# Attention, then two feed-forward layers, on one core: attention's second and third step change places

## The chip, the cores and the metric

The kernel runs on one core of a Trainium2 chip. The core has five engines that run side by side: TensorE (PE: matmuls, with a weight load, PEld, before each), VectorE (DVE), ScalarE (ACT), GpSimd (POOL) and SyncE (SP, which here only issues DMAs). Each works through its own list of instructions in order and waits for the others by semaphores. The metric is the device time of one execution in microseconds (us).

## The reference

The first layer is causal attention with a bias from a running sum; `x` then goes through a gated layer with a maximum over three products, and through one with a product of two.

```python
B, H, S, D = 4, 8, 576, 64
scores = q @ k.T / sqrt(D)
cum = cumsum(maximum(s, 0))
scores = where(causal, -1e9, scores + minimum(-(cum_q - cum_k), 0))
attn = exp(scores - max); attn /= (sum(attn) + 1e-9)
x = (attn @ v) as 2304 tokens x 512
h = maximum(maximum(x @ w1, x @ w2), x @ w3)      # 512 x 768, three times
x = h @ w_out                                     # 768 x 512
x = ((x @ w_a) * (x @ w_b)) @ w_out2              # 512 x 1536, twice; 1536 x 512
```

## The kernel before

**Steps.** Attention is cut into eight steps: for each of the four batches a short step (queries and keys 0 to 255) and a long one (queries 256 to 575, keys 0 to 575). A step has four pairs of heads, p0 to p3. A pair's scores go through a chain of engines: PE writes them to one of two PSUM buffers (`ps_s`); DVE adds the mask and takes the row's minimum (L398); ACT takes the exponential and its sum (L405); DVE takes the reciprocal (L409, L410); POOL scales the rows (L415); PE transposes them (`ft`, `t`, `tj`); ACT copies them out (`PF`); PE multiplies by the values (`fpv`); ACT and DVE split the result into a rounded part and a remainder (`Xh`, `Xl`).

**Two kinds of scores.** In the first three steps of the order the scores are plain: one full fp32 matmul over 64 rows and two more that carry the bias (`f` and `fj`, line 466; a long step has per pair four `f` of 384 or 512 columns, and two halves `fj` of a tile that both heads share). In all other steps they are split (`s`, `sj`, lines 422 to 457): operands are rounded to fp32r, the remainders and the bias stand in further rows, and two fp32r matmuls make a score. The operands stand in `QA1`, `QA2`, `KB1`, `KB2`, of which there is one each, and are written for every pair by `split_qk`: `KB` rounded on ACT and subtracted on DVE (64x1152), `QA` on ACT, POOL and DVE (64x640). A pair's loads (`kraw`, `qvraw`, two buffers each) are asked for two pairs ahead, when the value product of a pair is done; the queries and values share one buffer.

**The gated layer as filler.** While attention runs, PE fills its time with the gated layer of earlier steps: 18 gate units (`g`, line 592, 12 matmuls each of 256 or 320 columns) and four output units (`o`, line 620, 18 matmuls each) for every step. They need the step's `X` and the 24 chunks of weights, each of which is loaded by SP (512 KB), turned from 64-bit into fp32 by ACT (L241) and DVE (L244, L245), rounded on POOL (`hg`, `ho`) and subtracted on DVE (`lg`, `lo`). Three staging buffers hold chunks on their way.

**What sets the order.** The program makes a list (`stream`) of pieces with positions: an attention step takes one unit of position, gate and output units, and weight conversions, have positions of their own. Pieces are emitted by position, with priorities, and a scheduler then fixes each engine's order. After attention comes the rest of the gated layer and the last layer (line 1086), with PE as its chief engine.

Of the kernel before, what the change touches and what calls it, by code (L numbers as in the profile page):

```python
# [9 lines left out]
F32R = mybir.dt.float32r  # L10
# [19 lines left out]
def kernel(  # L30
# [29 lines left out]
    P = 128  # L60
# [9 lines left out]
    NPLAIN = 3  # L70
# [198 lines left out]
    def fetch_w1(key):  # L269
        if key in w1_t:  # L270
            raw = wst.tile([P, WC, 2], I32, tag="wst", name="wraw")
        else:
            if key == w1_keys[NPRE - MF]:
                wst.release()
                w1o.append(
                    tc.alloc_tile_pool(name="w1o", bufs=1, side="left", reuse_waits="tile")
                )
            w1_tiles(w1o[0], [key])
            raw = w1o[0].tile([P, WC, 2], I32, tag="raw", bufs=1, name="wraw")
        if key[0] == "g":  # L280
            src = (w1, w2, w3)[key[1]][key[2]]
        else:
            src = wo[key[1]]
        fetch_w(raw, src)
        w1_raw[key] = raw
# [11 lines left out]

    def is_plain(b, R):


        return 2 * b + R < NPLAIN

# [335 lines left out]
    pairs = [(b, R, p) for b in range(B) for R in range(2) for p in range(NP)]  # L638
# [133 lines left out]
    def x_tiles(stp):  # L772
        if stp not in xt:
            while todo and todo[0][0] <= stp - 2 and todo[0][1] < 3 * MF:
                todo.pop(0)[2]()
            R = stp % 2
            n = N1 if R else Q0
            xt[stp] = [
                mp.tile([P, KC, n], F32R, tag=f"X{c}{R}", bufs=1, name=f"X{c}")
                for c in "hl"  # L780
            ]
        return xt[stp]
# [6 lines left out]
    M0, M1 = 0.7, 0.1  # L789
    W0, W1, W2 = (0.09, 0.27, 0.34, 0.38), 1.3, 1.8  # L790
    for stp in range(nsteps):
        b, R = divmod(stp, 2)
# [9 lines left out]
        tot = sum(c for c, _ in units)  # L802
        acc = 0.0
        m0 = stp + 1 + (M0 if stp == 0 else M1)
        m1 = stp + 2 + M1
        for n, (c, fn) in enumerate(units):
            todo.append((stp, n, fn))
            stream.append((m0 + (m1 - m0) * acc / tot + 1e-6, 0, m_next))
            acc += c
# [12 lines left out]
    ng = 3 * MF  # L822
    for j in range(ng):
        w_at = W0[j] if j < 3 else W0[3] + (W1 - W0[3]) * (j - 3) / (ng - 3)
        stream.append((w_at, 200, w_next))
    for j in range(MF):
        stream.append((W1 + (W2 - W1) * j / MF, 200, w_next))
    stream.sort(key=lambda e: e[0])
    for pos, off, fn in stream:
# [5 lines left out]
        else:  # L835
            fn()
    moe = [(1, m_next) for _ in range(len(todo))]
# [702 lines left out]
```

## Time and profile before

| what | value |
| --- | --- |
| median of 3 timed runs | 921.25 us (918.19 to 922.32) |
| the profiled execution's own time, and its span | 915.72 us, 913.9 us |
| PE busy | 900.2 us, 98% |
| DVE busy | 592.2 us, 65% |
| ACT busy | 378.9 us, 41% |
| POOL busy | 225.7 us, 25% |

The span is the profiled part; 1.8 us of that execution lie around it. PE counts as busy from the start of a matmul to its modelled end, and matmuls overlap in the pipeline, so a PE that waits a little between matmuls still shows as busy. What it really does is seen by the distance from one start to the next.

### The profile page before, as it was taken

The page shows a single profiled execution, that of the slowest core. Times are in us where ns is not written, and L with a number is a line of the kernel's source. Part 1 is how long each engine was busy: PE and PEld are TensorE (multiplying, and loading weights), DVE is VectorE, ACT ScalarE, POOL GpSimd, SP SyncE. Part 2 cuts the span into 40 slices and gives each one's busy share as a digit, 9 for nine tenths or more (in the row PEclk, how much of TensorE's full clock was granted, in tenths as well). Part 3 has the DMA queues.
Part 4 walks back from the last instruction along what each step waited for, and adds up shares of the span by engine and source line. Part 5 has one row for each costly group of instructions (what it writes and reads, how often), then busy time and mean ns, then how long its engine had stood idle before and what let it go on. Part 6 is the DMA issues. An engine that isn't in the chain of part 4 may idle for free.

```text
span 913.9 us, 17151 instructions
## 1 busy us (share of the span) xinstructions
PE 900.2 (98%) x6296; PEld 849.0 (93%) x6296; DVE 592.2 (65%) x1407; ACT 378.9 (41%) x879; POOL 225.7 (25%) x328
## 2 busy tenths in 40 slices
PE   7999999999999999999999999999999999999998
PEld 7677899989999989999899999999999998999998
DVE  4798535554465544555369567767675868996874
ACT  4665634555446564465433332322322222423321
POOL 6654302222123221232122102111111212321211
PEclk9999999999999999999999999999999999999999
DMA  5665332313223132221143214444443243254331
GB/s 169 224 202 175 90 87 73 98 42 101 70 85 97 43 91 80 85 85 54 41 149 134 88 53 155 152 150 145 144 159 107 107 146 122 77 165 158 117 116 47
DMA packets 55212, 102.36 MB, mean 112 GB/s; under 512 B 5736, under 2 KB 39432, under 8 KB 55128
## 3 DMA queue, kind: packets, MB, share of 16 engines
q1 hardware_dynamic: 50520, 96.54, 33.4%
q10 hardware_dynamic: 4608, 4.72, 1.6%
q8 instruction: 50, 0.82, 0.4%
q14 instruction: 34, 0.28, 0.1%
HBM read 77.29 MB, written 23.94 MB: 111 GB/s over the span
## 4 chain that ended last, share of the span: by engine, by line
PE 90%; DVE 4%; DMA 3%; issue 1%; SPq 1%; ACT 1%; POOL 0%; DVEq 0%; ACTq 0%; POOLq 0%
PE g L592 25%; PE X L1086 23%; PE Z L1086 11%; PE o L620 9%; PE Y L1086 6%; PE fpv L531 5%; PE t L545 3%; PE f L466 2%; PE s L422 2%; PE s L423 1%; DVE slot L897 1%; PE ft L508 1%; DMA wraw<-in_moe_w_dram 1%; PE tj L558 1%; PE sj L456 1%
## 5 line engine op out<-in xcount | busy, mean ns | idle before, releaser
L592 PE MATMUL g<-Xh,hg 128*128 128x256 f32 (+1 forms) x576 | 174.8, 305 | 0.5 <-ACT xo L625 0.5
L592 PE MATMUL g<-Xl,hg 128*128 128x256 f32 (+1 forms) x576 | 173.4, 301 | 0.0
L592 PE MATMUL g<-Xh,lg 128*128 128x256 f32 (+1 forms) x576 | 173.2, 301 | 0.0
L592 PEld LDWEIGHTS g<-Xh,hg 128*128 128x128 f32 x576 | 108.5, 189 | 4.4 <-issue 1.6
L592 PEld LDWEIGHTS g<-Xl,hg 128*128 128x128 f32 x576 | 108.9, 189 | 2.5 <-issue 1.4
L592 PEld LDWEIGHTS g<-Xh,lg 128*128 128x128 f32 x576 | 108.8, 189 | 1.2 <-issue 0.9
L1086 PE MATMUL X<-xh,wh 128*128 128x384 f32 x288 | 97.5, 339 | 1.5 <-ACT u L1127 0.6
L1086 PE MATMUL X<-xl,wh 128*128 128x384 f32 x288 | 96.9, 336 | 0.0
L1086 PE MATMUL X<-xh,wl 128*128 128x384 f32 x288 | 96.9, 337 | 0.0
L88 POOL TENSOR_SCALAR wh<-wval 128x256 fp32r<-128x256 f32 x84 | 41.5, 503 | 190.5 <-DVE wval L891 141.8
L1086 PE MATMUL X<-woh,slot 128*128 128x256 f32 x432 | 81.1, 281 | 0.5 <-ACT ob L1129 0.5
L415 POOL TENSOR_SCALAR P<-P,rs 128x128 f32<-128x128 f32 (+2 forms) x80 | 50.1, 631 | 91.4 <-DVE rs L410 75.0
L601 DVE TENSOR_TENSOR hf<-g,hf 128x256 f32<-128x256 f32 (+1 forms) x96 | 43.5, 453 | 41.5 <-PE g L592 39.4
L897 DVE TENSOR_TENSOR slot<-hraw,slot 128x768 fp32r<-128x768 f32 x60 | 60.5, 1031 | 14.9 <-POOL slot L88 13.7
L1086 PEld LDWEIGHTS X<-woh,slot 128*128 128x128 f32 x432 | 68.0, 189 | 0.7 <-ACT ob L1129 0.7
L897 DVE TENSOR_TENSOR u<-Z,u 128x384 f32<-128x384 f32 x72 | 39.6, 552 | 44.5 <-ACT u L1129 34.0
L405 ACT ACTIVATE P<-P,nm 128x128 f32<-128x128 f32 (+2 forms) x80 | 46.5, 582 | 32.7 <-DVE nm L398 27.1
L1086 PE MATMUL X<-wol,slot 128*128 128x256 f32 x216 | 60.1, 280 | 0.0
L620 PE MATMUL o<-hh,lo 128*128 128x256 f32 (+1 forms) x192 | 58.0, 306 | 0.0
L620 PE MATMUL o<-hl,ho 128*128 128x256 f32 (+1 forms) x192 | 57.8, 303 | 0.0
L620 PE MATMUL o<-hh,ho 128*128 128x256 f32 (+1 forms) x192 | 57.0, 302 | 0.3 <-ACT xo L625 0.3
L398 DVE CUSTOM_DVE_ANT_0 P<-s,maskJ 128x128 f32<-128x128 f32 (+2 forms) x80 | 40.5, 514 | 25.7 <-PE s L423 16.7
(165 smaller groups left out, 2255.9 us busy)
## 6 DMA issues: line engine op xcount, KB each, us to landing
hT<-u SPq DMA_DIRECT2D x72, 192.0 KB
hraw<-hT SPq DMA_DIRECT2D x36, 384.0 KB
wraw<-in_moe_w_dram SPq DMA_DIRECT2D x18, 512.0 KB
wraw<-in_moe_w_out_dram SPq DMA_DIRECT2D x18, 512.0 KB
qvraw<-in_qv_dram SPq DMA_DIRECT2D x12, 640.0 KB
kraw<-in_kT_dram SPq DMA_DIRECT2D x24, 288.0 KB
wraw<-in_moe_w_a_dram SPq DMA_DIRECT2D x12, 512.0 KB
wraw<-in_moe_w_b_dram SPq DMA_DIRECT2D x12, 512.0 KB
```

What stands on the lines that cost most here:

```text
L88: nc.gpsimd.tensor_scalar(o, i, scale, 1.0, op0=ALU.mult, op1=ALU.mult)
L398: nc.vector.tensor_tensor_reduce(pt[:, c0 : c0 + w], v_, m_, -scale, first, op0=ALU.add, op1=ALU.min, accum_out=nm[:, i : i + 1],)
L405: e_ = nc.scalar.activation(pt[:, c0:c1], pt[:, c0:c1], AF.Exp, bias=first, scale=-1.0, accum_out=sm[:, g : g + 1],)
L415: nc.gpsimd.tensor_scalar(pt[:, c0:c1], pt[:, c0:c1], rs[:, g : g + 1], 1.0, op0=ALU.mult, op1=ALU.mult,)
L422: nc.tensor.matmul(ps, QA1[:, qs], KB1[:, h, ksl], start=True, stop=False)
L531: nc.tensor.matmul(ps[h * D : h * D + D, c0:n], w, x, start=(t == 0), stop=(t == len(mm[h]) - 1),)
L545: nc.tensor.transpose(ps[:, j * P : j * P + P], pt[:, j * P : j * P + P], ident)
L592: nc.tensor.matmul(ps[:, :n], w[:, kk, :], x[:, kk, :], start=(i == 0), stop=(i == len(mm) - 1),)
L601: st["V"] = nc.vector.tensor_tensor(hf, ps[:, :n], hf, op=ALU.max)
L620: nc.tensor.matmul(ps[:, :n], w[:, c, :], x[:, m, :n], start=(i == 0), stop=(i == len(mm) - 1),)
L897: return {"V": nc.vector, "P": nc.gpsimd}[e].tensor_tensor(o, a, b, op=op)
L1086: nc.tensor.matmul(ps[:, :n], w, x, start=(first and i == 0), stop=(i == len(mm) - 1), skip_group_check=not first,)
```

## The change

The first four steps run in the order batch 0 short, batch 1 short, batch 0 long, batch 1 long (before: batch 0 short, batch 0 long, batch 1 short, batch 1 long). Plain scores are used for the two short steps alone, so batch 0's long step is now split like the other long steps. The buffers of `X` are named after the step's place in the list and not its kind, and each is 320 columns wide. Gate and output units of the first three steps get positions from a table (`FILL`), and the weight conversions stand at new positions: the fourth to sixth from 0.68 (before from 0.38), the next seven over the second step, the last eleven over the first half of the third. The last two weight chunks' staging buffer gets a pool of its own, which is released when attention ends.

```diff
-    NPLAIN = 3
@@ fetch_w1
-        if key in w1_t:
+        if w1_keys.index(key) < len(w1_keys) + NPRE - MF:
...
+                for nm in ("w1o", "w1r"):
...
     def is_plain(b, R):
-        return 2 * b + R < NPLAIN
+        return R == 0 and b < 2
...
-    pairs = [(b, R, p) for b in range(B) for R in range(2) for p in range(NP)]
+    steps = [(0, 0), (1, 0), (0, 1), (1, 1)]
+    steps += [(b, R) for b in range(2, B) for R in range(2)]
+    pairs = [(b, R, p) for b, R in steps for p in range(NP)]
...
-                mp.tile([P, KC, n], F32R, tag=f"X{c}{R}", bufs=1, name=f"X{c}")
+                mp.tile([P, KC, n], F32R, tag=f"X{c}{stp % 2}", bufs=1, name=f"X{c}")
...
-    M0, M1 = 0.7, 0.1
-    W0, W1, W2 = (0.09, 0.27, 0.34, 0.38), 1.3, 1.8
+    M1 = 0.1
+    FILL = [(1.05, 2.22, 2.45, 2.65), (2.65, 3.12, 3.12, 3.3), (3.3, 3.9, 3.9, 4.1)]
...
+        elif j < 6:
+            w_at = 0.68 + 0.105 * (j - 3)
+        elif j < 13:
+            w_at = 1.0 + 0.143 * (j - 6)
+        else:
+            w_at = 2.0 + 0.057 * (j - 13)
...
+    w1o[1].release()
```

The engines' lists show three places. First DVE, in the first short step, around the fourth weight conversion (`wraw`, whose load comes late): before, it stands between the first half of the sixth score tile, `F_431`, and the reciprocal of the tile before.

```order
L398 ISA F_431,nm<-f_430,maskJ 128x128
L398 ISA nm 128x1
L244 TENSOR_SCALAR wraw<-wraw 128x512
L410 RECIPROCAL rs<-rs 128x2
L92 TENSOR_TENSOR Xl<-fpv,Xh 128x256
L398 ISA F_431,nm<-f_430,maskJ 128x256
```

In the changed kernel the same tile is `F_408`, and the conversion's first instruction stands one tile later.

```order
L399 ISA F_408,nm<-f_407,maskJ 128x128
L399 ISA nm 128x1
L411 RECIPROCAL rs<-rs 128x2
L91 TENSOR_TENSOR Xl<-fpv,Xh 128x256
L399 ISA F_408,nm<-f_407,maskJ 128x256
L399 ISA nm 128x1
L91 TENSOR_TENSOR lg_0_147<-wraw,hg_0_146 128x512
L410 TENSOR_SCALAR rs<-sm 128x2
L399 ISA F_460,nm<-f_459,maskJ 128x128
L399 ISA nm 128x1
L411 RECIPROCAL rs<-rs 128x2
L243 TENSOR_SCALAR wraw<-wraw 128x512
```

The reciprocal, the remainder and the tile's second half have moved ahead of the conversion.

Second PE, in batch 0's long step, at the change from the third pair to the fourth. Before, the next pair's scores (`fj`) and the transposes stand among gate matmuls and need no operand of their own.

```order
L592 MATMUL g<-Xh,lg_5_175 128x256
L466 MATMUL fj<-kraw,qvraw 64x288 x2
L592 MATMUL g<-Xh,hg_5_174 128x256
L545 MATMUL t_958<-ident,F_894 128x128 x4
L592 MATMUL g<-Xl,hg_5_174 128x256
L592 MATMUL g<-Xh,lg_5_175 128x256
```

After, a pair's last scores (`s_1581`), few output matmuls and the last transposes stand ahead of the next pair's joint scores `sj`.

```order
L423 MATMUL s_1581<-KB_138,QA_140 128x384
L424 MATMUL s_1581<-KB_139,QA_141 128x384
L546 MATMUL t_1574<-ident,P_1491 128x128 x3
...
L546 MATMUL t_1600<-ident,P_1503 128x128 x4
...
L546 MATMUL t_1621<-ident,P_1537 128x128 x4
L457 MATMUL sj<-KB_138,QA_140 128x288
L458 MATMUL sj<-KB_138,QA_140 128x288
```

In the two gaps stand six and three output matmuls; the scores `sj` now read `KB` and `QA`, which must be rewritten after `s_1581`.

Third DVE, in the same step of the changed kernel, one pair earlier: `P_1315` is the last tile but one of the second pair, `KB` belongs to the third.

```order
L399 ISA P_1315,nm<-s_1312,maskJ 128x512
L399 ISA nm 128x1
L91 TENSOR_TENSOR Xl<-fpv,Xh 128x320
L411 RECIPROCAL rs<-rs 128x1
L91 TENSOR_TENSOR lo_183<-wraw,ho_182 128x512
L91 TENSOR_TENSOR KB_139<-kraw,KB_138 64x1152
L410 TENSOR_SCALAR rs<-sm 128x1
L399 ISA P_1347,nm<-s_1344,maskJ 128x384
L399 ISA nm 128x1
L411 RECIPROCAL rs<-rs 128x1
L243 TENSOR_SCALAR wraw<-wraw 128x512
L376 SCALAR_TENSOR_TENSOR QA_140<-qvraw,QA_140 64x2x320
```

The split of the operands and the weight conversions now stand in one list with the softmax of the same step; before, this step had no split.

## Rows read from the trace of the kernel before

**Rows 1.** Windows by stage: busy us and instructions of each engine, clock, DMA.

```profile
31.60:91.80 60.20, 60.04 (x397) 43.63 (x397) 52.99 (x156) 37.79 (x93) 31.51 (x40) 1.00 0.63 204
91.80:148.70 56.90, 56.90 (x408) 50.88 (x406) 25.69 (x93) 27.01 (x79) 13.24 (x24) 1.00 0.31 87
148.70:460.00 311.30, 311.30 (x2380) 289.16 (x2380) 158.93 (x516) 164.77 (x417) 75.74 (x114) 1.00 0.26 76
```

**Rows 2.** Timeline of PE in batch 0's long step: start, duration, instruction.

```profile
47.71 0.71 PE L466 MATMUL fj<-kraw,qvraw 66*64 66x288 f32 x4
48.34 0.39 PE L592 MATMUL g<-Xh,hg 128*128 128x256 f32 x1
...
50.11 0.28 PE L592 MATMUL g<-Xh,lg 128*128 128x256 f32 x1
50.23 0.28 PE L592 MATMUL g<-Xh,hg 128*128 128x256 f32 x1
...
53.95 1.02 PE L466 MATMUL f<-kraw,qvraw 66*128 66x512 f32 x2
54.80 0.39 PE L545 MATMUL t<-ident,F 128*128 128x128 f32 x2
```

**Rows 3.** Timeline of PE in batch 1's long step, whose scores are split.

```profile
154.18 0.40 PE L422 MATMUL s<-KB,QA 128*128 128x512 f32 x1
...
154.66 0.30 PE L592 MATMUL g<-Xh,hg 128*128 128x320 f32 x1
...
163.53 0.29 PE L456 MATMUL sj<-KB,QA 128*128 128x288 f32 x1
163.66 0.29 PE L457 MATMUL sj<-KB,QA 128*128 128x288 f32 x1
```

**Rows 4.** Groups of PE instructions, 31.6 to 91.7 us: count, busy, mean ns, idle.

```profile
L592 PE MATMUL g<-Xh,hg 128*128 128x256 f32 x72 | 21.7, 312 | 0.0
...
L545 PE MATMUL t<-ident,F 128*128 128x128 f32 x42 | 7.0, 275 | 0.2 <-POOL F L415 0.2
...
L531 PE MATMUL fpv<-PF,qvraw 128*64 128x320 f32 x24 | 4.6, 447 | 0.0
```

**Rows 5.** Timeline of all engines, 24 to 34 us; in brackets the idle time before.

```profile
27.89 0.43 DVE L244 TENSOR_SCALAR wraw<-wraw 128x512 int32<-128x512 int32 x1 [3.09 <-DMA wraw<-in_moe_w_dram]
...
28.23 0.16 DVE L410 RECIPROCAL rs<-rs 128x2 f32<-128x2 f32 x1
...
32.24 0.39 PE L592 MATMUL g<-Xh,hg 128*128 128x256 f32 x1
```

**Rows 6.** Groups of DVE instructions, 31.6 to 92 us: the weight conversions.

```profile
L245 DVE SCALAR_TENSOR_TENSOR wraw<-wraw 128x512 int32<-128x512 int32 x18 | 13.3, 739 | 0.7 <-ACT wraw L241 0.5
L92 DVE TENSOR_TENSOR lg<-wraw,hg 128x512 fp32r<-128x512 f32 x15 | 10.9, 725 | 1.9 <-POOL hg L88 1.6
L244 DVE TENSOR_SCALAR wraw<-wraw 128x512 int32<-128x512 int32 x18 | 9.1, 504 | 2.7 <-DMA wraw<-in_moe_w_dram 1.5 <-DMA wraw<-in_moe_w_out_dram 1.2
```

**Rows 7.** Groups of DVE instructions, 0 to 340 us: operand split and score rows.

```profile
L92 DVE TENSOR_TENSOR KB<-kraw,KB 64x1152 fp32r<-64x1152 f32 x8 | 11.4, 1425 | 4.8 <-ACT KB L81 4.8
L398 DVE CUSTOM_DVE_ANT_0 P<-s,maskJ 128x512 f32<-128x512 f32 x16 | 11.0, 690 | 6.1 <-PE s L423 3.8 <-PE tj L558 2.1
...
L375 DVE SCALAR_TENSOR_TENSOR QA<-qvraw,QA 64x640 fp32r<-64x640 f32 x8 | 7.6, 946 | 2.7 <-ACT QA L81 2.6
```

**Rows 8.** Timeline of all engines, 187 to 199 us: a pair's queries arrive.

```profile
187.69 2.42 PE L531 MATMUL fpv<-PF,qvraw 128*64 128x320 f32 x20
...
190.19 0.34 SPq L343 DMA_DIRECT2D qvraw<-in_qv_dram  x1
...
194.32 0.72 POOL L88 TENSOR_SCALAR QA<-qvraw 64x640 fp32r<-64x640 f32 x1 [4.09 <-DMA qvraw<-in_qv_dram]
```

**Rows 9.** Group of POOL instructions, 31.6 to 92 us: scaling of 512 columns.

```profile
L415 POOL TENSOR_SCALAR F<-F,rs 128x512 f32<-128x512 f32 x6 | 6.8, 1140 | 4.8 <-DVE rs L410 4.8
```

**Rows 10.** The same work on POOL, 340 to 460 us.

```profile
L415 POOL TENSOR_SCALAR P<-P,rs 128x512 f32<-128x512 f32 x8 | 6.1, 767 | 8.6 <-DVE rs L410 4.8 <-PE o L620 2.2 <-PE s L423 0.9
```

More of the change, by code (lines that the diff above doesn't have):

```diff
@@ L274, in fetch_w1 @@
                 wst.release()
[L275 to L279, printed above, removed]
+                for nm in ("w1o", "w1r"):
+                    w1o.append(
+                        tc.alloc_tile_pool(name=nm, bufs=1, side="left", reuse_waits="tile")
+                    )
+                    if nm == "w1o":
+                        w1_tiles(w1o[0], w1_keys[NPRE - MF :])
+            raw = w1o[1].tile([P, WC, 2], I32, tag="raw", bufs=1, name="wraw")
         if key[0] == "g":
@@ L775, in x_tiles @@
                 todo.pop(0)[2]()
-            R = stp % 2
-            n = N1 if R else Q0
+            n = N1 if steps[stp][1] else Q0
             xt[stp] = [
-                mp.tile([P, KC, n], F32R, tag=f"X{c}{R}", bufs=1, name=f"X{c}")
+                mp.tile([P, KC, n], F32R, tag=f"X{c}{stp % 2}", bufs=1, name=f"X{c}")
                 for c in "hl"
@@ L786, in m_next @@
             todo.pop(0)[2]()
-    M0, M1 = 0.7, 0.1
-    W0, W1, W2 = (0.09, 0.27, 0.34, 0.38), 1.3, 1.8
+    M1 = 0.1
+    FILL = [(1.05, 2.22, 2.45, 2.65), (2.65, 3.12, 3.12, 3.3), (3.3, 3.9, 3.9, 4.1)]
     for stp in range(nsteps):
-        b, R = divmod(stp, 2)
+        b, R = steps[stp]
         att = []
@@ L801 @@
         units = moe1_units(R, b, lambda stp=stp: x_tiles(stp))
[L802 to L805, printed above, removed]
+        m0 = stp + 1 + M1
+        g0, g1, o0, o1 = FILL[stp] if stp < 3 else (m0, m0 + 0.75, m0 + 0.75, m0 + 1)
+        ng = 3 * MF
         for n, (c, fn) in enumerate(units):
             todo.append((stp, n, fn))
-            stream.append((m0 + (m1 - m0) * acc / tot + 1e-6, 0, m_next))
-            acc += c
+            if n < ng:
+                at_ = g0 + (g1 - g0) * n / ng
+            else:
+                at_ = o0 + (o1 - o0) * (n - ng) / (len(units) - ng)
+            stream.append((at_ + 1e-6, 0, m_next))
     def tails():
@@ L820, in w_next @@
             load_w1(w1_pend.pop(0))
-    ng = 3 * MF
-    for j in range(ng):
-        w_at = W0[j] if j < 3 else W0[3] + (W1 - W0[3]) * (j - 3) / (ng - 3)
+    W0 = (0.09, 0.27, 0.34)
+    for j in range(len(w1_keys)):
+        if j < 3:
+            w_at = W0[j]
+        elif j < 6:
+            w_at = 0.68 + 0.105 * (j - 3)
+        elif j < 13:
+            w_at = 1.0 + 0.143 * (j - 6)
+        else:
+            w_at = 2.0 + 0.057 * (j - 13)
         stream.append((w_at, 200, w_next))
-    for j in range(MF):
-        stream.append((W1 + (W2 - W1) * j / MF, 200, w_next))
     stream.sort(key=lambda e: e[0])
```

## The prediction, made before the changed kernel ran

> **What bounds the kernel now.** I read the windows first. From 31.6 us on PE is busy nearly all the time, at a granted clock of 1.00 [rows 1]. Busy is not enough: in the pipeline a waiting PE still shows as busy. So I set the number of matmuls against the distance between starts. A gate matmul of 256 columns starts 0.12 us after the one before; a full fp32 score of 512 columns holds PE for 0.85 us (one of 384, by columns, 0.64), a half of the plain joint tile for 0.63 [rows 2]. From 31.6 to 91.7 us there are 216 gate matmuls (three groups of 72): 25.9 us. The group of transposes has 42, and 25 more are in three smaller ones: 67 at 0.11, 7.4 us. Six scores of 512, seven of 384 and eight joint halves make 5.1, 4.5 and 5.0. Two long value products (24 records of 320 columns, 12 each) take 2.4 each [rows 4, 8], two short ones together some 1.6. The sum is 54.3 us, and the stretch lasts 60.2 [rows 1]: PE loses 5.9 us there. DVE is busy for 52.99 of the 60.2 us, 88%, because of the weight conversions; in the next two windows it is busy for 45% and 51%, and there I take PE's losses as alike before and after. So the kernel is bound by PE's work, plus what PE waits in the first 92 us, plus a start in which it has little to do: the first gate matmul comes at 32.24 us [rows 5]. Any PE time saved without a new wait shortens the whole.
>
> **The change, part by part.**
>
> The scores of batch 0's long step. A pair now costs PE 2 x 0.64 + 2 x 0.85 + 2 x 0.63 = 4.24 us. Split, a score of 512 columns takes 0.48 (two matmuls), one of 384 then 0.36, and a joint half is four matmuls at 0.13, 0.53 us [rows 3]: 2 x 0.48 + 2 x 0.36 + 2 x 0.53 = 2.74. Four pairs: 4 x 1.5 = **6.0 us saved**. The Trainium skill, FP8 and Floating Point Precision, section TensorE Precision Notes, says that true fp32 goes through the array in four passes; counted so for each head, a joint half would take 2 x 4 x 288 columns at 2.4 GHz, 0.96 us, and the term would be an estimate of 8.7 us. The measured 0.63 decides: the two heads' halves are not counted one after the other.
>
> The start. In the first short step DVE sat idle for 3.09 us, until 27.89, before a weight conversion whose load had not landed; the reciprocal behind it ran at 28.23 [rows 5], and the remainder and a half tile behind that. In the new list they stand ahead of it. Not all of the 3.09 us comes back: on ACT the same conversion still stands ahead of the copy that the second pair's value product needs. Bounds 0 and 3.1; I take **1.3 us saved**, a little under the middle.
>
> The second short step, as filler's first home. Until batch 0's joint scores PE has 170 gate matmuls (20.4 us) and some 13 us of plain scores, transposes and value products. DVE has eight weight conversions in that time, each of three instructions, 0.74 + 0.73 + 0.50 less 0.08 for each, since the next one starts before the last one's record ends (28.23 against 27.89 + 0.43) [rows 5, 6]: 1.73 us, 13.8 together, and some 12.5 us of the rest. That is 80% of PE's 33 us, less than the 88% that went with a loss of a tenth. Waits between 0 and 3.3 us; I take 2.5, nearer to the stretch before.
>
> The long split step. This is where the gain can go. From the first pair's joint scores to the end of the output units PE has 46 gate and 72 output matmuls (14.2 us), scores (15 split ones and four joints, 10.6), 57 transposes (6.3) and three value products (7.3): 38.4 us. DVE has, by its list, nine weight conversions (15.6), three `KB` of 1.43 and three `QA` of 0.95 [rows 7], less the overlap 6.6; eight score tiles of 512 at 0.61, seven of 384 at about 0.48 and eight joint halves at about 0.41, 11.5; and some 6 us of reciprocals, remainders and gate maxima: 39.7 us. So DVE needs at least 1.3 us more than PE. At the 88% that it reached before, it needs 45.1, and PE waits 6.7. What is late next is seen by walking through the lists. There is one `KB` and one `QA`, so between a pair's last score and the next joint stand ACT's rounding and DVE's 1.43 us, and on DVE whatever is queued ahead; the reciprocals for the last tiles of the old pair are queued behind `KB`, so POOL's scaling and the last transposes wait for it too. Before, such a change was covered by many gate matmuls; now by nine output matmuls, 1.1 us, and transposes. At the third and fourth pair the queries add to it: their buffer is free when the value product two pairs back is done, and from the request (190.19) to the first use (194.32) is 4.1 us [rows 8], to which ACT's and DVE's `QA` add some 1.8, so 5.9; behind the second pair's value product PE has only 3.7 us of work. Adding up such waits with the durations above I get 4.4 us up to the first pair's value product, 1.8 at the third pair and 2.5 at the fourth, 8.7 in all; conversions are shorter when POOL is quiet, so I take **8.2**, between 1.3 and 11 (each of the eight last transposes and joints waiting 0.3 us longer).
>
> What I cost at nothing: the wider buffers of `X`, since the instructions use only the columns of the step; the plain loads of the second short step, which are smaller than those of the long one that they replace; the tail of the filler, since by the fourth step all eight steps' units stand where they stood. If the last is wrong, it would show as waits of PE after 150 us, where DVE is at 51% [rows 1]. The staging pool's release moves a buffer that nothing waits for there.
>
> The sum: -6.0 - 1.3 + (2.5 + 8.2 - 5.9) = -2.5 us, on the profiled execution's 915.72 us, so 913.2. That execution lies 5.5 us under the median of the timed runs, 921.25; by the same difference I predict **918.5** for the median, 0.3% less. About 0.5%, 4.6 us, is what a measurement of this kernel can tell from no change.
>
> **The rivals.**
>
> PE's waits stay small. The conversions leave the start, and DVE's 39.7 us need not bind if the scheduler has put into each gap what is ready: then the second short step loses 1 us and the long one 3, and the sum is -6.0 - 1.3 + (4 - 5.9) = -9.2, so 912. For it: before, PE lost only a tenth while DVE was 88% busy. Against it: then the step had no operands to rewrite. Between this and my sum lies a continuous scale; I give the half below about -4.6 us a chance of 0.35.
>
> The loads come late, and the change is slower. Queries, keys and weight chunks share SP's list, and a chunk's request there waits for a staging buffer that DVE frees; a pair's loads stand behind it. If each of the step's four joints waits 3 us longer than I have it, and the first value product after it, that is +13 us: 931. It decides when the step's waits pass 10.7 us, and by 0.5% at 15.3. For it: DMA engines are at 0.63 and 204 GB/s in the early window [rows 1], and the step asks for four pairs' full keys, queries and values besides nine chunks. Against it: that window fed DVE at the same rate with few waits for DMA in its groups [rows 6]. Chance 0.12.
>
> POOL and DVE slow each other. Scaling 512 columns took 1140 ns on POOL in the stretch where DVE was 88% busy, and 767 ns where it was not [rows 9, 10]. At the old pair's last transposes in the long step, which wait for POOL, it costs 0.37 us more than at the quiet rate at six tiles: +2 us, 920.5, no change still. The Trainium skill, GPSIMD Engine Reference, section 1. Specifications, says that GpSimd's SBUF interfaces are shared with VectorE; the trace agrees, with these two rows. I count it into the forecast's own range.
>
> That the change does not do what it says, with the scheduler putting the old order back, is out: the lists show `sj` in batch 0's long step.
>
> **How the numbers follow.** Forecast (a saving of 0 to 4.6 us, or a loss up to 3) 0.48; small waits 0.35; late loads 0.12; anything else, such as a change of the later steps by some us either way, 0.05. Faster by over 0.5%: small waits and a part of the rest, 0.38; slower by over 0.5%: late loads and a little, 0.13; within: 0.49. The forecast's own range is 916 to 922. The range for 8 in 10 leaves out the slower half of the late loads and the best of the small waits: 910.5 to 923.5.
>
> **What would show it.** In the changed kernel's profile: no `f` of 384 or 512 columns, and PE's groups of `s` and `sj` up by a third; the idle time of DVE before the fourth conversion gone, and the first gate at about 31 us; in the long step DVE at 85% or more and starts of PE further apart than 0.12 us at the joints of the second, third and fourth pair, with DVE's `KB` or `QA` as what came last. The prediction is wrong if that step's PE work takes 41 us or less (then it is the first rival), or 50 or more with waits for `qvraw` or `kraw`.

## The result, and the profile after

The changed kernel takes **927.77 us** (median of four, 927.55 to 929.16) where the kernel before took 920.22 beside it (918.19 to 922.32): ratio **1.0085**, interval 1.0058 to 1.0112. It is slower by about 7.5 us; 918.5 was forecast. Beside all later runs the kernel before took 917.0 to 917.7 us (medians), so this one ratio may be some 0.3% too low when it is set against those below. The two profiled executions lie 11.9 us apart (spans 925.8 and 913.9), and that distance is already there in batch 2's long step, whose second joint starts at 291.88 us and at 279.18 before.

Windows of the changed kernel, as in [rows 1]: length, busy us of PE, PEld, DVE, ACT and POOL, granted clock, DMA share, GB/s.

```profile
33.10:72.00 38.90, 36.26 (x276) 30.79 (x275) 34.26 (x102) 24.91 (x74) 20.98 (x30) 1.00 0.78 235
72.00:129.00 57.00, 47.34 (x300) 38.83 (x299) 43.84 (x127) 35.27 (x80) 25.16 (x30) 0.88 0.48 144
78.50:81.90 3.40, 3.40 (x14) 3.26 (x15) 3.27 (x7) 3.40 (x8) 3.04 (x3) 0.50 0.18 28
102.40:105.80 3.40, 3.27 (x15) 3.27 (x16) 2.09 (x7) 1.37 (x4) 1.32 (x3) 0.50 0.77 221
116.10:122.90 6.80, 5.61 (x24) 5.12 (x24) 4.13 (x12) 2.03 (x5) 1.41 (x3) 0.50 0.39 99
129.00:150.00 21.00, 21.00 (x173) 19.68 (x173) 9.58 (x29) 10.07 (x24) 3.33 (x5) 1.00 0.31 93
150.00:460.00 310.00, 310.00 (x2333) 289.34 (x2332) 156.31 (x502) 162.40 (x411) 72.22 (x110) 1.00 0.25 71
```

The first row is the second short step, the second is batch 0's long step to the end of the output units. The reader is to see three things. PE is idle for 9.7 us of the long step, where [rows 1] had it busy throughout. VectorE is busy for 43.84 of 57 us, 77%: it isn't the bound there. And TensorE's clock, 1.00 in every window of [rows 1], is granted at 0.50 (1.2 GHz instead of 2.4) in three stretches inside it.

Groups of PE, DVE and POOL in the long step (72 to 129 us, POOL to 130), as in [rows 4, 6, 7, 9]: count, busy, mean ns, idle before and what ended it.

```profile
L546 PE MATMUL t<-ident,P 128*128 128x128 f32 x42 | 8.4, 326 | 5.8 <-POOL P L416 5.8
...
L423 PE MATMUL s<-KB,QA 128*128 128x512 f32 (+1 forms) x15 | 6.4, 427 | 1.3 <-DVE nm L399 1.3
L457 PE MATMUL sj<-KB,QA 128*128 128x288 f32 x16 | 6.2, 398 | 0.9 <-DVE QA L376 0.9
...
L244 DVE SCALAR_TENSOR_TENSOR wraw<-wraw 128x512 int32<-128x512 int32 x9 | 7.3, 822 | 0.0
L91 DVE TENSOR_TENSOR KB<-kraw,KB 64x1152 fp32r<-64x1152 f32 x3 | 4.1, 1355 | 0.1
L243 DVE TENSOR_SCALAR wraw<-wraw 128x512 int32<-128x512 int32 x9 | 3.8, 434 | 2.3 <-DMA wraw<-in_moe_w_out_dram 2.3
...
L416 POOL TENSOR_SCALAR P<-P,rs 128x512 f32<-128x512 f32 x8 | 8.3, 1034 | 4.4 <-DVE rs L411 1.9 <-ACT xo L626 1.4 <-ACT PF L560 0.9
```

VectorE's durations are near those that the sum went by (`KB` 1355 ns against 1425, two instructions of a conversion 822 and 434 against 739 and 504). What is new stands at the end of the first row: the transposes `t`, with 0.2 us of idle time ahead of 42 of them in [rows 4], now have 5.8, all of it for GpSimd's scaled rows. Timeline of one such wait, in the second pair, from the request for the next pair's queries on:

```profile
92.98 0.33 SPq L344 DMA_DIRECT2D qvraw<-in_qv_dram  x1
...
97.50 0.15 DVE L411 RECIPROCAL rs<-rs 128x1 f32<-128x1 f32 x1
...
98.27 1.35 DVE L91 TENSOR_TENSOR KB<-kraw,KB 64x1152 fp32r<-64x1152 f32 x1
98.30 0.63 PE L621 MATMUL o<-hh,lo 128*128 128x256 f32 x3
...
99.30 0.92 POOL L87 TENSOR_SCALAR QA<-qvraw 64x640 fp32r<-64x640 f32 x1 [2.05 <-DMA qvraw<-in_qv_dram]
...
99.66 0.15 DVE L410 TENSOR_SCALAR rs<-sm 128x1 f32<-128x1 f32 x1
99.73 0.55 DVE L399 CUSTOM_DVE_ANT_0 P<-s,maskJ 128x384 f32<-128x384 f32 x1
...
100.20 0.16 DVE L411 RECIPROCAL rs<-rs 128x1 f32<-128x1 f32 x1
...
100.32 2.16 POOL L416 TENSOR_SCALAR P<-P,rs 128x512 f32<-128x512 f32 x2
...
101.30 0.66 PE L546 MATMUL t<-ident,P 128*128 128x128 f32 x4 [2.37 <-POOL P L416]
...
102.53 1.11 PE L546 MATMUL t<-ident,P 128*128 128x128 f32 x4 [0.58 <-POOL P L416]
```

PE's last output matmul ends at 98.93; then PE stands before four transposes for 2.37 us, until 101.30. Its list is taken in order, so what is queued behind them waits too. The row that they need is scaled by the first of the two scalings at 100.32. Its reciprocal had ended at 97.65, ahead of `KB` (scalings take their reciprocals in order, and this one is next); what it waited for stands before it in GpSimd's own list: the rounding of the next pair's queries, for which GpSimd waited 2.05 us, until 99.30. So behind this wait is a late load (6.3 us from the request to GpSimd's first use, where the prediction had 4.1). Only the second scaling's reciprocal (100.20) stood behind `KB`. In the third pair PE's output matmuls end at 113.95, and the transposes start at 116.34. There both causes end within 0.15 us of each other: GpSimd waits 1.49 us for the queries and rounds them until 115.25, and the reciprocal behind `KB` (113.31 to 114.67) ends at 115.40. By these rows, taking away either one alone would bring almost nothing. After it VectorE waits for a weight chunk, with the next pair's queries behind it:

```profile
113.34 0.34 SPq L229 DMA_DIRECT2D wraw<-in_moe_w_out_dram  x1
...
114.23 1.02 POOL L87 TENSOR_SCALAR QA<-qvraw 64x640 fp32r<-64x640 f32 x1 [1.49 <-DMA qvraw<-in_qv_dram]
...
115.24 0.16 DVE L411 RECIPROCAL rs<-rs 128x1 f32<-128x1 f32 x1
115.59 0.69 POOL L416 TENSOR_SCALAR P<-P,rs 128x512 f32<-128x512 f32 x1 [0.34 <-DVE rs L411]
...
116.34 1.11 PE L546 MATMUL t<-ident,P 128*128 128x128 f32 x4 [2.39 <-POOL P L416]
117.06 0.43 DVE L243 TENSOR_SCALAR wraw<-wraw 128x512 int32<-128x512 int32 x1 [1.67 <-DMA wraw<-in_moe_w_out_dram]
...
117.53 0.82 DVE L376 SCALAR_TENSOR_TENSOR QA<-qvraw,QA 64x640 fp32r<-64x640 f32 x1
...
118.40 0.61 PE L457 MATMUL sj<-KB,QA 128*128 128x288 f32 x1 [0.95 <-DVE QA L376]
118.81 0.44 PE L458 MATMUL sj<-KB,QA 128*128 128x288 f32 x1
119.05 0.44 PE L457 MATMUL sj<-KB,QA 128*128 128x288 f32 x1
```

The last two rows are at half clock: joint halves start 0.24 us apart, where those of 72.00 us (below) start 0.13 apart. In the second short step the longest wait is that of a gate for a weight conversion, whose load had come late (VectorE waited 1.12 us for it, until 65.41):

```profile
65.41 0.43 DVE L243 TENSOR_SCALAR wraw<-wraw 128x512 int32<-128x512 int32 x1 [1.12 <-DMA wraw<-in_moe_w_dram]
...
65.56 0.28 PE L593 MATMUL g<-Xl,hg 128*128 128x256 f32 x1
67.52 0.39 PE L593 MATMUL g<-Xh,lg 128*128 128x256 f32 x1 [1.69 <-DVE lg L91]
...
72.00 0.29 PE L457 MATMUL sj<-KB,QA 128*128 128x288 f32 x1
72.13 0.29 PE L458 MATMUL sj<-KB,QA 128*128 128x288 f32 x1
```

**How waits are counted below.** PE's matmuls of each kind in a stretch are multiplied by the distance of their starts when PE doesn't wait (gate or output of 256 columns 0.12, of 320 columns 0.15, transpose 0.11, `s` of 512 0.24 and of 384 0.18, `sj` 0.13, plain score of 512 0.43 per record and two records each, a joint half plain 0.63, value product 2.4 or 0.8); the rest of the stretch is waiting, and includes what is lost at half clock. Up to batch 1's first long joint, from 20 us on, the kernel before waits 11.5 us, the changed one 28.8: 9.2 ahead of batch 0's first joint (72.0) and 19.6 behind it. 17.3 more, less the 6.0 of work saved, is 11.3 of the 11.9. The counts are good to about 1 us: with slightly other distances ahead of 33 us, where PE also runs matmuls whose result nothing reads (`spin`), all values of the first part shift by some 2 us together.

### The profile page after: what moved, and what is told of

It is laid out like the page before. It is cut to its first block, busy times and chain, and to the rows that moved or that the text cites. A ratio compares the mean times of both kernels' runs of the same rounds, so it can differ in the third digit from the quotient of the medians.

```text
span 925.8 us, 17202 instructions
## 1 busy us (share of the span) xinstructions
PE 900.9 (97%) x6296; PEld 857.2 (93%) x6296; DVE 603.1 (65%) x1415; ACT 385.6 (42%) x887; POOL 229.9 (25%) x332
## 4 chain that ended last, share of the span: by engine, by line
PE 87%; DVE 5%; DMA 4%; issue 1%; POOL 1%; ACT 1%; SPq 0%; POOLq 0%; DVEq 0%; ACTq 0%
PE g L593 23%; PE X L1096 22%; PE Z L1096 11%; PE o L621 8%; PE Y L1096 6%; PE fpv L532 5%; PE t L546 2%; PE s L423 2%; PE s L424 2%; PE ft L509 1%; DVE slot L907 1%; PE f L467 1%; PE sj L457 1%; PE sj L458 1%; PE spin L150 1%
## 5 line engine op out<-in xcount | busy, mean ns | idle before, releaser
L416 POOL TENSOR_SCALAR P<-P,rs 128x384 f32<-128x384 f32 (+2 forms) x96 | 64.2, 673 | 120.5 <-DVE rs L411 86.4
L406 ACT ACTIVATE P<-P,nm 128x384 f32<-128x384 f32 (+2 forms) x96 | 57.2, 597 | 36.3 <-DVE nm L399 29.8
L907 DVE TENSOR_TENSOR slot<-hraw,slot 128x768 fp32r<-128x768 f32 x60 | 60.5, 1031 | 15.0 <-POOL slot L87 13.7
L399 DVE CUSTOM_DVE_ANT_0 P<-s,maskJ 128x384 f32<-128x384 f32 (+2 forms) x96 | 50.3, 531 | 23.3 <-PE s L424 15.6
L1096 PEld LDWEIGHTS X<-xh,wh 128*128 128x128 f32 x288 | 54.1, 188 | 3.0 <-ACT u L1137 1.1
```

The lines of the kernel that those rows point to most:

```text
L399: nc.vector.tensor_tensor_reduce(pt[:, c0 : c0 + w], v_, m_, -scale, first, op0=ALU.add, op1=ALU.min, accum_out=nm[:, i : i + 1],)
L406: e_ = nc.scalar.activation(pt[:, c0:c1], pt[:, c0:c1], AF.Exp, bias=first, scale=-1.0, accum_out=sm[:, g : g + 1],)
L416: nc.gpsimd.tensor_scalar(pt[:, c0:c1], pt[:, c0:c1], rs[:, g : g + 1], 1.0, op0=ALU.mult, op1=ALU.mult,)
L907: return {"V": nc.vector, "P": nc.gpsimd}[e].tensor_tensor(o, a, b, op=op)
L1096: nc.tensor.matmul(ps[:, :n], w, x, start=(first and i == 0), stop=(i == len(mm) - 1), skip_group_check=not first,)
```

## The experiments

Ratios are to the kernel before on the same chip, three rounds each. Waits are of the profiled execution: ahead of batch 0's first long joint from 20 us on (a), and from there to batch 1's first long joint (b). v1 and y5 lose 5 to 8 us more than their counts show; both also wait some 4 us more behind the counted stretch.

| kernel | ratio (interval) | a | b | sum |
|---|---|---|---|---|
| before | 1 | | | 11.5 |
| changed | 1.0085 (1.0058-1.0112) | 9.2 | 19.6 | 28.8 |
| x1_conv_as_before | 1.0073 (1.0058-1.0088) | 12.8 | 10.8 | 23.6 |
| x2_plain01 | 1.0082 (1.0065-1.0099) | 9.6 | 10.6 | 20.2 |
| x3_no_dve_conv | 1.0064 (1.0049-1.0079) | 11.5 | 12.5 | 24.0 |
| x4_split_in_place | 1.0094 (1.0078-1.0110) | | | 25.6 |
| y1_cover | 1.0124 (1.0108-1.0140) | 10.8 | 18.3 | 29.1 |
| y3_kb_after_rs | 1.0228 (1.0213-1.0244) | 10.9 | 27.8 | 38.7 |
| y5_no_rewrite | 1.0114 (1.0091-1.0136) | 18.9 | 8.9 | 27.8 |
| y7_plain_cover | 1.0060 (1.0037-1.0084) | 10.5 | 9.2 | 19.7 |
| x8_plain01_conv | 1.0064 (1.0039-1.0089) | 12.0 | 11.0 | 23.0 |
| z1_no_low | 1.0061 (1.0043-1.0079) | 14.6 | 10.4 | 25.0 |
| z2_short_rewrite | 1.0048 (1.0033-1.0063) | 12.5 | 9.6 | 22.1 |
| v1_conv_alone | 1.0228 (1.0211-1.0245) | | | 26.3 |
| q1_no_chunk_loads | 1.0073 (1.0048-1.0097) | 8.6 | 19.0 | 27.6 |
| q2_no_dve_conv_all | 1.0176 (1.0146-1.0206) | 13.7 | 21.1 | 34.8 |
| q3_conv_and_rewrite | 1.0076 (1.0048-1.0104) | 12.9 | 12.7 | 25.6 |
| n2_before_nudged | 1.0008 (0.9997-1.0019) | | | 13.3 |
| n4_after_nudged | 1.0146 (1.0119-1.0173) | 11.3 | 17.8 | 29.1 |
| y8_conv_and_cover | 1.0077 (1.0059-1.0095) | 13.1 | 10.8 | 23.9 |

**The parts of the change alone.** Conversions back in their old places (x1); batch 0's long step plain again (x2); both (x8), which leaves the new order of steps, the filler's places and the buffers; the split alone in the old order (x4); the conversions alone in the old order (v1).

```diff
 x2: -        return R == 0 and b < 2
     +        return (R == 0 and b < 2) or (b, R) == (0, 1)
 x4: -        return 2 * b + R < NPLAIN
     +        return R == 0 and b < 2
 x1: W0, W1, W2 and their loops as in the kernel before; x8 = x1 and x2
 v1: W0 and its loop as in the changed kernel
```

> The changed kernel with the weight conversions placed as in the kernel before (the last gate chunk by 1.27 steps, the last output chunk by 1.8), all else changed as it was. In the changed kernel PE needs 57 us from batch 0's first joint scores (72.0 us) to the end of the output units (128.9), for 38.4 us of work. Theory 1: the nine weight conversions in that step keep VectorE from the scores' reductions, reciprocals and low parts. Then the long step comes down to 45 us or less, the second short step gets longer by 4 to 6 us, and the time is 918 to 922. Theory 2: the rewriting of KB and QA between pairs, with only nine output matmuls as cover, costs it whatever else VectorE does. Then the long step stays above 52 us and the time is 927 or more.

> The changed kernel, but batch 0's long step computes its scores plainly again, in the new place and with the new conversions: 6 us more PE work there, no KB and QA there. Theory 1 (conversions): VectorE loses 6.6 us of KB and QA but keeps the 15.6 us of conversions; the waits fall by about the 6 us that the work grows, and the time is 925 to 929. Theory 2 (rewriting without cover): the waits fall from 18 to about 6 us, and the time is 919 to 923. In both no stretch of that step is at half the clock.

> The kernel before with one part of the change alone: batch 0's long step has split scores, in its old place (second), with the conversions and the filler as they were. PE's work falls by 6 us. Theory 1: VectorE, 88% busy in that stretch, gets 6.6 us of KB and QA on top, and PE waits 6 us or more longer: 920 to 926. Theory 2: 72 gate matmuls lie beside it as cover, and the rewriting is hidden: 914 to 917.

> The changed order of steps and filler alone: batch 0's long step is plain and the weight conversions stand where the kernel before has them. Theory L (the change loses in two places that have nothing to do with the split scores: gates in the second short step that outrun the weight conversions, and the last weight chunks, whose late loads hold VectorE and ScalarE up in the long step): both are gone here, and the time is within 0.2% of the kernel before. Theory O (the order of the steps itself costs it): 0.6% or more over the kernel before, as with the new conversions.

> The kernel before with the new places of the weight conversions alone (three by 0.34 steps, three by 0.9, seven by 1.9, the last eleven from 2.0 to 2.6). Its gates begin at 1.7 steps, so some conversions are called for by a gate and come at once. Theory L: the gates wait for them and the time is 0.4% or more over the kernel before. If the new places only take work from VectorE where it is busy, the time is the same or 0.2% less, with the first gate up to 1.3 us earlier.

x1 came out between its two theories: the long step's waits fell, those ahead of it rose. x2 lies at the edge of theory 1's time, but with 6.8 us at half clock in its long step, which neither theory had. x4 (926.2 us) is at the upper end of theory 1's time, v1 as theory L.

Each part alone is slower than the kernel before, and they don't add. The new order with plain scores costs 0.82%, and with the old conversion places still 0.64%, though PE's work is that of the kernel before: theory O, not L. The order was not tried apart from the filler's new places and the buffers, so the 0.64% belongs to the three together. The split in the old place costs 0.94%: 14.1 us of waits for 6.0 of work. On top of the new order the ratios tell no cost (x2 against the changed kernel, x8 against x1), the times 0.2% to 0.3%. The conversions alone are worst; the old order has its gates and outputs earlier, and outputs wait for weights there (`o` for VectorE's low part 2.6 us, for GpSimd 1.8), which is a part of v1's waits. x8's profiled execution was its slowest (929.15 us, seven from 919.47), with 3.4 and 10.2 us at half clock; its waits are high by that.

In x2's long step a weight chunk holds VectorE and ScalarE up, the reciprocal stands behind it, and PE behind that; then the plain joint waits for its own rows:

```profile
109.77 0.43 DVE L243 TENSOR_SCALAR wraw<-wraw 128x512 int32<-128x512 int32 x1 [2.15 <-DMA wraw<-in_moe_w_out_dram]
...
110.29 0.16 DVE L411 RECIPROCAL rs<-rs 128x1 f32<-128x1 f32 x1
...
111.39 0.66 PE L546 MATMUL t<-ident,F 128*128 128x128 f32 x4 [2.30 <-POOL F L416]
...
114.23 0.75 PE L467 MATMUL fj<-kraw,qvraw 66*64 66x288 f32 x2 [2.18 <-DMA qvraw<-cq]
```

**VectorE's work taken away.** Conversions 13 to 23 without their three instructions on VectorE (x3), all from 3 on (q2; in both the low part is a copy on ScalarE); the low parts of `KB` and `QA` left out (z1) or the whole rewriting done for 64 columns (z2), both on x1; q2 and the short rewriting (q3); no rewriting (y5).

```diff
 x3: +            if thin: rnd("P", hi, f(Hw)); rnd("A", lo, f(Hw)); return
     (thin: index of the chunk >= 13; q2: >= 3)
 z2: +        if (b, R) == (0, 1) and p > 0:
     +            nk = nq = 64; kn, qn = kn[:, :, :64], qn[:, :, :64]
     (q3 = q2 and this; z1 leaves out the two VectorE instructions instead)
 y5: -        if split_pair(i):
     +        if split_pair(i) and i not in (2 * NP + 1, 2 * NP + 2, 2 * NP + 3):
```

> The changed kernel, leaving out VectorE's three instructions of the weight conversions 13 to 23 (the value isn't put together, and the low part is a copy by ScalarE); loads, ScalarE's first and GpSimd's instruction stay. Eleven conversions less, about 19 us of VectorE in the second half of the second short step and in the long step. Theory 1: the waits of the long step fall from 18 us to 6 or less, the half clock there goes, and the time is 913 to 917. Theory 2: the joints still wait for KB and QA, 13 us or more of waits stay, and the time is 922 to 927.

> The changed kernel with the conversions placed as before, leaving out VectorE's low parts of KB and QA (1.4 and 0.9 us) for pairs 2 to 4 of batch 0's long step; the roundings on ScalarE and GpSimd, the tails and the loads stay. With these low parts this placement took 0.73% more than the kernel before, with 13 us more of PE's waits. If VectorE's 6.6 us are what the split costs there, the waits fall by 6 us or more: at most 0.1% over the kernel before. If it is the chain (a joint that can't start before the roundings, which can't start before the last score), the time falls by 2 us at most: 0.5% over or more.

> The changed kernel with the conversions placed as before, and the rewriting of KB and QA for pairs 2 to 4 of batch 0's long step done for the first 64 columns of each head alone: every instruction, wait and load stays, each takes a third of the time or less. If the length of the rewriting (4 us from the last score to the joint) is what the split costs, 8 us or more of waits go, and the time is below that of the kernel before by 0.2% or more. If the loads of the operands or the softmax's chains bind, it stays 0.5% over it or more.

> The changed kernel, leaving out the rewriting of KB and QA (rounding, low parts, tails) for pairs 2 to 4 of batch 0's long step, which compute their scores with the first pair's operands. Three KB, three QA on VectorE (6.6 us less), their roundings on ScalarE and GpSimd, and the waits of the joints for them are gone; scores, conversions and filler stay. Theory 2: the waits of the long step fall from 18 to 8 us or less and the time falls by 8 us or more. Theory 3: the softmax's chains still wait with nothing beside them, and the time falls by 4 us or less.

> The changed kernel, leaving out VectorE's three instructions of the conversions 3 to 23 (the low part is a copy by ScalarE, as in the run that left out 13 to 23); the loads stay. Theory V: the waits of the second short step fall from 7 to 3 us or less, and those of the long step to some 12, as they did without conversions 13 to 23; the time is 0.2% over the kernel before or less. Theory D: the second short step keeps 6 us or more, and the time stays 0.5% over it.

> The run without VectorE's conversions 3 to 23, and with the rewriting of KB and QA for pairs 2 to 4 of batch 0's long step done for 64 columns of each head alone. VectorE has some 35 us less to do in 33 to 130 us. Theory V: both of its loads together were the long step's waits: they fall from 20 to 8 us or less, and the time is 0.4% or more below the kernel before (the 6 us of PE work come out as forecast). Theory D: waits for loads and for the softmax's chains stay, 12 us or more in the long step, and the time is that of the kernel before or more.

z1 (0.61%) and x3 (922.7 us) took what their second theories had, z2 fell between its two (0.48%). In y5 the long step's waits fell to 8.9 us, near theory 2's 8, but the time rose, which neither theory had. q2 and q3 are as theory D.

None reaches the kernel before. Windows of q3, its second short step and its long one:

```profile
33.00:77.00 44.00, 37.61 (x288) 31.85 (x286) 15.82 (x71) 31.88 (x88) 15.11 (x30) 1.00 0.78 241
77.00:141.00 64.00, 59.65 (x414) 49.69 (x415) 29.45 (x114) 43.51 (x103) 21.75 (x33) 0.95 0.42 128
```

VectorE (the third number) is busy 36% and 46%, and PE still waits 12.9 (from 20 us on) and 12.7 us. So VectorE's load alone does not set these waits. But ScalarE took over a copy per chunk and is at 72% and 68%, and GpSimd waits 15.0 us for ScalarE's part of the conversions between 33 and 140 us: the run takes load from one engine and puts it on another, and can't clear VectorE by itself. In the long step conversions and rewriting do count: with the conversions elsewhere or off VectorE, or without the rewriting, b falls from 19.6 to 9 to 13 (x1, x3, y5), but taking away more brings no further fall. And part of it comes back ahead of the step. In y5 keys of the next pairs, free to be requested early, stand in SyncE's list between and ahead of weight chunks, and a gate waited 4.3 us for a chunk. That the keys delayed it is argued from this order, not tried:

```profile
65.14 1.11 SPq L346 DMA_DIRECT2D kraw<-in_kT_dram  x2
66.35 0.52 SPq L229 DMA_DIRECT2D wraw<-in_moe_w_dram  x1
67.47 1.11 SPq L346 DMA_DIRECT2D kraw<-in_kT_dram  x2
68.67 0.54 SPq L229 DMA_DIRECT2D wraw<-in_moe_w_dram  x1
...
69.58 0.28 PE L593 MATMUL g<-Xl,hg 128*128 128x256 f32 x1
73.10 0.43 DVE L243 TENSOR_SCALAR wraw<-wraw 128x512 int32<-128x512 int32 x1 [5.02 <-DMA wraw<-in_moe_w_dram]
...
74.18 0.58 PE L593 MATMUL g<-Xh,lg 128*128 128x256 f32 x1 [4.32 <-DVE lg L91]
```

**Loads, cover, places in the list.** No loads for chunks 3 to 21 (q1); the second step's gates brought into the long step (y1, y7 with plain scores, y8 with the old conversion places); the rewriting behind the last reciprocal (y3).

```diff
 q1: +        if 3 <= n_ < len(w1_keys) + NPRE - MF:
     +            w1_raw[key] = kept[n_ % 3]; return
 y1: FILL = [(1.05, 2.22, 2.28, 2.4), (2.4, 3.1, 3.12, 3.3), ...]
     w_at = 1.9 + 0.038 * (j - 13)
     (y7 = y1 and x2; y8 = x1 and y1's FILL)
 y3: +                with tc.issue_after(done_sm[-1][1]):
                          split_qk(b, p, R, *nat_of[i][:2])
```

> The changed kernel, leaving out the loads of the weight chunks 3 to 21: their conversions work on the first three chunks' buffers in turn, so that ScalarE, VectorE and GpSimd do the same work and wait for the same buffers. In the changed kernel PE waits 7.0 us from the first gate (33.1) to batch 0's first joint (72.0), and 19.6 from there to batch 1's first joint (138.3). Theory D (DMA: the chunks come late, and hold up VectorE, ScalarE and the gates): the first falls to 3 or less, the second by 5 or more, and the time falls by 8 us or more, to the time of the kernel before or less. Theory V (VectorE's work binds): the waits fall by 3 us at most in all.

> The changed kernel with the gates of the second step's units brought forward into batch 0's long step (from 2.4 steps on instead of 2.65, behind batch 0's output units at 2.28 to 2.4 instead of 2.45 to 2.65, the last eleven conversions 0.1 to 0.3 of a step earlier), so that more gate matmuls lie beside its joints. Theory 2 (the rewriting of KB and QA as such binds it): the long step still waits 13 us or more in all, and the time falls by 3 us at most, to 925 or more where the changed kernel takes 928. Theory 3 (the chains of the softmax are as long as everywhere, and the step has too little filler to lie over them): the waits behind 90 us fall from 13 to 5 us or less, no half clock is left there, and the time falls by 7 us or more, to 921 or less.

> The changed kernel with batch 0's long step plain again and with the second step's gates brought forward as in the kernel with more cover. With plain scores alone the changed kernel took 0.8% more than the kernel before, though its work is the same; it waited 2.7 us for weight conversions at 65 us and 4.8 us in the fourth pair for a weight chunk and rows of cq. Theory 3: the latter is filled by gates and 4 us or more come back, to 0.4% over the kernel before or less. If it is the order of loads on SyncE, the waits stay: 0.7% or more over it.

> The changed kernel with the conversions placed as in the kernel before and with the second step's gates brought forward into batch 0's long step. The first alone took 0.73% more than the kernel before, with 9.9 us of waits in the second short step and 11 in the long one. If gates beside the long step's chains cover them now that no conversion stands there, 4 us or more of the 11 go: 0.3% over or less. If the transposes still block PE in front of gates that stand behind them in its list, it stays at 0.6% or more.

> The changed kernel with the rewriting for pairs 2 to 4 of batch 0's long step put behind the last reciprocal of the pair before, on every engine; nothing else is asked to move. If the reciprocals that stand behind KB's 1.4 us and QA's 0.9 us on VectorE are what PE waits for (the last transposes waiting for GpSimd's scaling), the two waits of 2.5 us ahead of transposes go and the time falls by 3 us or more. If the joint is what matters, it comes later, waits of PE move from the transposes to the joints, and the time is the same or longer.

q1 is nearer to theory V than to D: its waits fell by 1.2 us in all. y1's time rose; y7 (0.60%) fell between its two. y8 is as the transposes that block PE would have it, y3 as its second case.

Without the chunk loads the second short step keeps 5.0 of its 7.0 us of waits and the long step 19.0 of 19.6: loads are a share of the first and hardly of the second. More gates in the long step don't cover its waits (18.3; beside the old conversion places 10.8 with them and 10.8 without): too little filler is not the cause as I had it. In y1 and q1 GpSimd does not wait for queries in the long step at all, and the waits are still 18.3 and 19.0: late queries stand behind the two longest waits of the changed kernel, alone or with another cause, but where they aren't late other waits fill the place. No run takes away the queries' loads alone, or puts their rounding behind the scaling in GpSimd's list. Putting reciprocals ahead of `KB` made it worse: PE waited for GpSimd's rows 9.9 us in ten places instead of 5.8 in four.

**A nudge.** One number of each kernel changed, which alters only the order dealt to the engines.

```diff
 n2: -M0, M1 = 0.7, 0.1      +M0, M1 = 0.68, 0.1        (kernel before)
 n4: -0.057 * (j - 13)       +0.055 * (j - 13)          (changed kernel)
```

> The kernel before with M0 0.68 instead of 0.7: nothing in the work changes, but some 120 of PE's rows and 20 of VectorE's come in another place. If a newly dealt order costs by itself what the runs so far show, it is 0.4% or more slower. If the cause is the order of the steps and the split, the time is within 0.2% of the kernel before.

> The changed kernel with the last eleven conversions 0.055 steps apart instead of 0.057: nothing in the work changes, some 185 of PE's rows come in another place. If the order dealt decides, the time differs from the changed kernel's (0.85% over the kernel before) by 0.3% or more either way. If not, it is 0.7 to 1.0% over the kernel before.

The kernel before doesn't notice. The changed one, nudged, took 1.46% over it, from two pairs of executions: 927.88 and 928.26 us, as without the nudge, and 932.29 and 932.69, at a mean clock of 0.987 instead of 0.990. So differences of some tenths of a per cent between its variants shouldn't be read closely.

## Why the prediction was wrong

Two sums end a little off, which changes nothing: 2.5 us off 921.25 is 918.75, not 918.5, and the estimate by four passes is 8.6 us, not 8.7.

**The scores: right.** `sj` halves start 0.13 apart and `s` pairs 0.23 and 0.24 (74.60 to 74.83): 2.74 us a pair as costed, and with 6.0 us off the 17.3 more waits the spans come out within 0.6 us.

**The start: wrong, by 2.2 us.** The idle time ahead of the fourth conversion is gone (it runs at 29.05 with none), but the first gate comes at 33.12, not at 31: the second pair's value product begins at 31.03 instead of 30.11, and the first pair's already at 23.64 instead of 22.89. DVE's idle time was not on PE's path there. The 0.88 us of delay against the kernel before need not be the change's doing: the clock over the first 20 us was 0.84 there and 0.91 before. n2, the kernel before with another order later on, has as long a stretch at half clock in its start (6.8 us) and its first gate at 32.87; x2, with the change's start and as little half clock as the kernel before (3.4 us), has it at 33.06.

**The second short step: mis-sized.** By the prediction's own count, 33 us of work, it waits 5.9 us (38.9 from 33.12 to 72.00); 2.5 were taken, 3.3 was the bound. That bound was the kernel before's loss in its long step, and nothing made it one.

**The long split step is the step that failed.** 38.4 us of work took 57 (72.00 to 128.95), so 18.5 us of waits (half clock's loss included), where 8.2 were taken and 11 was the upper bound. "At the 88% that it reached before, it needs 45.1" turned VectorE's busy time into PE's waits. VectorE reached 77%, where 85% or more was to be the sign, and with VectorE at 46% (q3, which puts more on ScalarE) the waits of the step were still 12.7 us. What PE waits for are chains through all engines, a score on PE, its row minimum on VectorE, exponential on ScalarE, reciprocal on VectorE, scaling on GpSimd, transposes on PE, each hop behind what stands ahead in that engine's list; the busy share of one engine doesn't measure them. The walk through the lists (8.7 us) saw the places, `KB`, the reciprocals behind it and the late queries, and undercounted them: pair by pair, to batch 1's first joint, 4.7, 6.4, 6.0 and 2.5 us were lost. It had the queries arrive after 4.1 us and hold up the joint; they took 6.3, and their rounding stands in GpSimd's list ahead of the old pair's scaling, so they held up the old pair's transposes as well.

**Left out altogether: the clock.** Behind the long waits TensorE is granted 1.2 GHz for 3.4, 3.4 and 6.8 us. The matmuls that started in these 13.7 us are 6.3 us of work at the distances of full clock, so half clock took at most some 6 us of the 18.5. In the kernel before there is no such stretch between 20 us and the end of its span. How much it cost is not shown. The changed kernel's four executions took 927.58, 929.16, 927.96 and 927.55 us at mean clocks of 0.989, 0.989, 0.992 and 0.994: the last had some 9 us less of half clock than the first, and the same time. Over the executions of all kernels, each kernel against its own mean, 1 us more of half clock goes with some 0.3 us more time, by an estimate from their times and clocks; waits, which come with it, are in that figure. And it is not the whole loss: x1 and x3 have none in these steps, and are 0.73% and 0.64% slower.

**What I costed at nothing** held in one point and failed in another. The tail is as before: the waits from batch 1's long step to 290 us differ by less than half a us. But the sum gave the new order of steps no term of its own, and x8 shows it, with the filler's places and the buffers, to cost 0.64% with the same work and the same conversion places.

**The rivals.** Small waits: no, the step took 57 us where 41 was the limit. Late loads: 18.5 us is beyond that rival's 15.3, its time was nearly right (931 for 927.8), and the sign named for it came: 50 us or more, with waits for `qvraw` (2.05 and 1.49 us on GpSimd). Its mechanism is there in part: the two longest waits are for GpSimd's rows, and GpSimd had waited for late queries ahead of both. But it isn't the whole: joints waited 0.95 us at most and not 3 each, without 19 of 24 chunk loads the time stays at 1.0073, and where GpSimd waits for no queries (q1, y1) the step loses as much. GpSimd and VectorE slowing each other: 1034 ns for 512 columns against 767 in [rows 10], so 2.1 us at eight tiles if all of it reached PE; but one tile of 2.34 us makes most of the mean (the other seven take 0.85), and no run takes it out.

**What stays open.** Shown is where the time goes, and that the split alone, the conversions alone, and the new order with its filler and buffers each cost time. Not shown is why the new order leaves some 20 us of waits whatever else is taken away (x2, y7, z2), where the old one has 11.5, and whether it is the order or the filler's new places. That the planner's list, dealt by estimated durations, puts PE's transposes too early for these chains is argued, not tried. No variant beat the kernel before.

## What to carry to other kernels

Don't turn the busy share of the busiest engine into waits of another: walk the chain that an in-order list must stand and wait for, and take what it cost in the same kind of step. On every engine of the chain ask what stands ahead in its list and what load that waits for. When two causes end at nearly the same time, taking away one shows nothing, as with the queries and `KB` here. And where TensorE's waits come close together, half clock may follow; what it adds to the time was not settled here.

## What the runs showed of the hardware

GpSimd's scaling of 512 columns, 0.77 us on average between 340 and 460 us [rows 10], took 2.34 us once, at 80.56, while VectorE's `QA` and `KB` ran (80.15 to 82.42): a tripling. It is not so each time: the two scalings at 100.32, beside another `QA` (100.72 to 101.92), took 2.16 us together. The Trainium skill, GPSIMD Engine Reference, section 1. Specifications, names contention of GpSimd's SBUF interfaces with VectorE's instructions of two SBUF inputs; both of these have two, and the row agrees.

```profile
80.56 2.34 POOL L416 TENSOR_SCALAR P<-P,rs 128x512 f32<-128x512 f32 x1
```

The half clock came each time behind a stretch in which PE had done little, and this need not be one long wait: ahead of 102.4 us PE was idle for 2.37 us, ahead of 78.5 for 0.76, 0.53 and 0.55 us, one shortly after the other. Not every wait brings it: x1's 2.22 us up to 95.03 had none behind it. Apart from the start it came in none of these kernels between 145 us and the last 2 us of the span, and not in the same places from kernel to kernel. Executions of one program differ in it: x8's ran from 919.47 us (mean clock 0.996) to 929.15 (0.989), the changed kernel's, at 0.989 to 0.994, only from 927.55 to 929.16.
